# First routing round of a fused attention and MoE kernel: float digits, split counts, a table of zero matmuls, and a new order of the experts' work

## The chip, the cores and the metric

One core of a Trainium2 chip runs the whole program. The metric is the device time in microseconds, the median of the runs shown; the profile is one further execution, whose trace gives every duration used below. TensorE is called PE, VectorE DVE, ScalarE ACT, GpSimd POOL and SyncE SP, as in the rows.

## The reference, cut to what matters

```python
# attention: 4 batches, 8 heads, 768 positions, 64 wide; sink of 4 keys and a window of 128
attn = softmax(mask(q @ k.T / 8)) @ v
x = attn.transpose(0, 2, 1, 3).reshape(3072, 512)
logits = x @ w_gate                      # 3072 tokens, 8 experts
order = argsort(-logits.flatten())
for idx in order:                        # greedy, capacity 384 for each expert
    tok, e = idx // 8, idx % 8
    if assigned[tok] >= 0 or counts[e] >= 384: continue
    assigned[tok] = e; counts[e] += 1
for e in range(8):
    out[assigned == e] = relu(x[assigned == e] @ w1[e]) @ w2[e]     # 512 -> 1024 -> 512
```

The greedy loop is done in eight rounds. In each the expert that fills up first is found, with the threshold at which its 384th token is taken; its tokens leave the pool, and the round hands over an expert number and 384 row numbers.

## The kernel before

The first stretch of the program is attention over 24 chunks of 128 positions, in an order written out by hand (`SEQ`). It leaves the rows x in DRAM and the logits `L` (128 partitions x 24 chunks x 8 experts) in SBUF. `Moe.side` puts the first operations of the first routing round, over the first 18 of the 24 columns, into that order as `pr0` to `pr16`.

The second stretch is planned: `graph` adds every instruction of the eight rounds (`phase`, classes R0 to R7), of the gathers and transposes of rows (`rows`, G and X), of the weights (`weights`, L, H, W) and of the two matmul layers (`mlp`, M and N) to a `Graph`, each with a cost and with what it reads and writes. `Graph.order` is a list scheduler: it takes the ready instruction of best rank, shifted by a number for each class from the table `BIAS`, within a window `WIN`. Each engine then runs its instructions strictly in the order that comes out. `run` emits them.

A round (`phase`, L420) looks for the threshold digit by digit. The best logit of each token is made into a sortable integer by `prep` (L376): `v` (L381) is the maximum, `vm` adds a penalty for tokens already taken, `f` and `s` (L386, L388) make the integer, `di` (L390 to L398) and `df` (L399) its digits, `w`, `mx` and `oh` (L385 to L393) the one-hot best expert. There are six steps, `STEPS`, two with 64 digit values and four with 32 (numbered 0 to 5 below: 64, 64, 32, 32, 32, 32). In each, `compare` (L356, L359) sets `cmp` to digit >= grid value for all 24 columns; `gather` (L375) counts for each expert, by matmuls with `cmp` as weights and `oh` as the moving operand, into the PSUM bank `pr`. DVE compares the counts with 384 (`odd`, `two`, `odd`, `i`: L458 to L463), one matmul `dp` (L467) sums over the partitions, and DVE reads it as the digit `P` (L469) and subtracts it (`xb`, L470; `x` and `y`, L450 to L452). With 32 values the layout before puts four column groups in one count, 6 matmuls of 128 weights and 32 columns, and the two halves of the result need the extra pair `odd`, `two` (L458, L459). After step 5 come the mask `M` (L482), running counts `sc` (L485), the ranks (L488, L489), `q` (L493), then the slot of each token in its expert's list, compared with 64 low values (`lo`, L498, L356) and six 64-wide edges in fp32 (L505, L509, L510), a last count (`pick`, L375), and the row numbers `idx` (L517 to L520). POOL gathers three times 128 rows with them (L557), PE transposes them (L565), ACT and DVE split them in a high and a low part `xh`, `xl` (L567, L568), and the first layer starts (L578, L586 for the first two column blocks, L581 for the others; the second layer is L597).

While PE waits in the first round it runs matmuls of zeros (`warm`, L418): `WARM` gives the number before each count, into the same bank `pr` as the count, and `run` adds more in the gaps of its own plan, into `ph`.

Weights come in 64 chunks of 512 KB over two raw buffers (`raw`, L548): ACT copies the high part `wh` (L550), DVE makes the low part `wl` (L552), and only then is the raw buffer free. Chunk 2 of the first expert also waits for the gathered rows.

The lines that put zeros ahead of a count before the change:

```python
for n,(sh,m) in enumerate(STEPS):
    ...
    def counts(n=n,m=m,cnt=cnt,z=z,h=h,j=j):
        if first: self.warm(cnt,WARM[n])
        self.gather(cnt,j,m,self.oh,k)
```

Of the kernel before, what the change touches and what calls it, by code (L numbers as in the profile page):

```python
# [233 lines left out]
CAP=384  # L234

RUN=[(4,0)]*2+[(2,2)]*6
# [70 lines left out]
class Moe:  # L307
# [4 lines left out]
    def __init__(self,ctx,tc,L,idn):  # L312
        nc=tc.nc; self.tc=tc; self.nc=nc; self.L=L; self.idn=idn
# [20 lines left out]
        for n,dt in (('v',F32),('vm',F32),('f',I32),('s',I32),('mx',F32),('y',F32),('sl',F32),('m3',F32),('lo',I16),('si',I16),('x0',F32),('x1',F32),('xb0',BF),('xb1',BF)): setattr(self,n,t([128,NC],dt,n))  # L334
# [4 lines left out]
        self.M=t([128,2,NC],BF,"M"); self.xae=t([128,2,NC],F32,"xae"); self.sc=t([128,2*NC],BF,"sc"); self.q=t([128,2,NC],F32,"q"); self.c4=t([128,NC,7],F32,"c4"); self.edge=t([128,6],F32,"edge")  # L339
        for j in range(6): g.memset(self.edge[:,j:j+1],64.0*j+63.5)  # L340
        self.R=t([128,NC,6],F32,"R"); self.R3=t([128,NC,6],F16,"R3")
# [21 lines left out]
    def gather(self,out,j,m,y,k,dt=BF):  # L363

        z=128//m; U=RUN[k][m<64]; n=y.shape[2]; l=[]
        if U:
            for b in range(0,NC//U,z):
                q=min(z,NC//U-b)
                st=self.cmp[j][:,b*m*U:(b+q)*m*U].bitcast(dt).rearrange("p (x u) -> p u x",u=U); mv=y[:,b*U:(b+q)*U].rearrange("p (j u) e -> p u j e",u=U)
                l+=[(q*m,q*n,st[:,u],mv[:,u]) for u in range(U)]  # L370
        else:
            st=self.part(j,m).bitcast(dt); mv=y.rearrange("p (j c) e -> p c j e",j=z)
            l=[(128,z*n,st[:,:,c],mv[:,c]) for c in range(NC//z)]
        l=[l[0]]+[x for x in l if x[0]<128]+[x for x in l[1:] if x[0]==128]
        for i,(r,w,a,b) in enumerate(l): self.nc.tensor.matmul(out[0:r,0:w],a,b,start=i==0,stop=i==len(l)-1)  # L375
    def prep(self,k,a,b):  # L376
# [13 lines left out]
            (u(n/2),lambda: V.tensor_scalar(di[:,5],s,-2**31,26,op0=OP.bitwise_xor,op1=OP.logical_shift_right),'s','di5'),  # L390
            (u(n/2),lambda: V.tensor_scalar(di[:,0],s,-2**31,20,op0=OP.bitwise_xor,op1=OP.logical_shift_right),'s','di0'),
            (u(n/2),lambda: V.tensor_copy(self.xb0[:,c],di[:,5]),'di5','xb0'),
            (u(8*n),lambda: V.tensor_tensor(self.oh[:,c],w,wide(mx),OP.is_equal),'w1 mx','oh'),  # L393
            (u((56 if RUN[k][0]==2 else 32)*n),lambda: self.compare(0,self.xb0,64,a,b,k),'xb0','cmp0'),
# [21 lines left out]
    def warm(self,bank,n):  # L416

        for _ in range(n): self.nc.tensor.matmul(bank[:,128:512],self.onesb,self.grid[:,0:16,:].rearrange("p m c -> p (m c)"),start=True,stop=True)  # L418

    def phase(self,g,k):  # L420
# [7 lines left out]
        if not last:  # L428
# [3 lines left out]
            if a<NC:  # L432
                for c,fn,r,w in self.prep(k,a,NC): v(c,fn,r,w)
            xb=(self.xb0,self.xb1); xs=(self.x0,self.x1); x,xn=self.df[:,0],'df'
            for n,(sh,m) in enumerate(STEPS):
                cnt,bn=bank(); j=n%2; cn=f'cmp{j}'; z=128//m; h=NC//z
                if n: v(u(NC*m/(1.15 if RUN[k][m<64]==2 else 2)),lambda j=j,m=m: self.compare(j,xb[j],m,0,NC,k),f'xb{j}',cn)
                def counts(n=n,m=m,cnt=cnt,z=z,h=h,j=j):
                    if first: self.warm(cnt,WARM[n])

                    self.gather(cnt,j,m,self.oh,k)
                e({0:62*h if m==64 else 52*h,2:27*h,4:35*h}[RUN[k][m<64]]+(100 if first else 0),counts,cn+' oh'+(' m0go' if (k,n)==(1,1) else ''),bn,f'cnt{n}')
# [13 lines left out]
                if z==2: top,tn=cnt[0:64,0:E],bn  # L456
# [10 lines left out]
                e(60,lambda z=z,dp=dp,wt=wt: nc.tensor.matmul(dp[:,0:E],wt,self.i8[z//4],start=True,stop=True),f'i8{z//4}',bn,f'dp{n}')  # L467
# [36 lines left out]
        v(u(NC),row0,'M0','c40')
        v(u(6*NC),lambda: V.tensor_tensor(c4[:,:,1:7],sl[:,:,None].to_broadcast([128,NC,6]),self.edge[:,None,:].to_broadcast([128,NC,6]),OP.is_ge),sn,'c4')  # L505
        oj=0; on=f'cmp{oj}'
        ip,bn=bank()
        v(u(NC*(56 if RUN[k][0]==2 else 32)),lambda: self.compare(oj,self.lo,64,0,NC,k,OP.is_equal,F16),'lo',on)
        v(u(6*NC),lambda: V.tensor_tensor(R,c4[:,:,0:6],c4[:,:,1:7],OP.subtract),'c40 c4','R')  # L509
        v(u(6*NC),lambda: V.tensor_tensor(self.R3,R,self.tid[:,:,None].to_broadcast([128,NC,6]),OP.mult),'R','R3')  # L510
        def pick():
            if first: self.warm(ip,WARM[6])
            self.gather(ip,oj,64,self.R3,k,F16)
# [100 lines left out]
    def run(self):  # L614
# [114 lines left out]
```

## Time and profile before

| | |
|---|---|
| three runs | 478.36, 478.58, 485.38 us |
| median | 478.58 us |
| profiled execution | 480.82 us, of which the span of the trace is 479.1 us |
| busy over the span | PE 442.8 us (92%), DVE 372.9 us (78%), ACT 227.2 us (47%), POOL 153.9 us (32%) |

Times in rows are counted from the start of the span; 1.72 us of the profiled execution lie outside it. A row of the timeline gives the start, the duration, the engine, the line, the operation, what it writes and reads, and in square brackets the idle time of the engine before it with what ended it. Merged rows end in xN and cover from the first start to the last end.

### The profile page before, as it was taken

The page shows a single profiled execution, that of the slowest core. Times are in us where ns is not written, and L with a number is a line of the kernel's source. Part 1 is how long each engine was busy: PE and PEld are TensorE (multiplying, and loading weights), DVE is VectorE, ACT ScalarE, POOL GpSimd, SP SyncE. Part 2 cuts the span into 40 slices and gives each one's busy share as a digit, 9 for nine tenths or more (in the row PEclk, how much of TensorE's full clock was granted, in tenths as well). Part 3 has the DMA queues.
Part 4 walks back from the last instruction along what each step waited for, and adds up shares of the span by engine and source line. Part 5 has one row for each costly group of instructions (what it writes and reads, how often), then busy time and mean ns, then how long its engine had stood idle before and what let it go on. Part 6 is the DMA issues. An engine that isn't in the chain of part 4 may idle for free.

```text
span 479.1 us, 14064 instructions
## 1 busy us (share of the span) xinstructions
PE 442.8 (92%) x5464; PEld 366.4 (76%) x5468; DVE 372.9 (78%) x1147; ACT 227.2 (47%) x647; POOL 153.9 (32%) x297
## 2 busy tenths in 40 slices
PE   9899898999864989999999999999999999999994
PEld 5587786877741578778879879878987889988983
DVE  5799898899886889988999989988878986463210
ACT  4988788789600153353344244335234345363110
POOL 5696667669800200411321211122031033011001
PEclk9999999899985699999999999999999999999999
DMA  8647658475620552572474463364346166664001
GB/s 280 204 139 217 214 180 258 136 220 160 197 73 0 176 156 89 175 234 74 129 224 132 136 216 134 110 200 153 110 136 189 73 203 229 190 194 153 0 23 44
DMA packets 44875, 73.79 MB, mean 154 GB/s; under 512 B 3592, under 2 KB 21256, under 8 KB 44808
## 3 DMA queue, kind: packets, MB, share of 16 engines
q1 hardware_dynamic: 40536, 59.78, 39.8%
q0 software_dynamic: 3840, 12.59, 7.7%
q8 instruction: 43, 0.70, 0.6%
q10 hardware_dynamic: 432, 0.52, 0.4%
q14 instruction: 24, 0.20, 0.1%
HBM read 60.28 MB, written 12.60 MB: 152 GB/s over the span
## 4 chain that ended last, share of the span: by engine, by line
PE 51%; DVE 27%; DMA 8%; ACT 6%; issue 5%; POOLq 0%; POOL 0%; SPq 0%; DVEq 0%; ACTq 0%
PE ph L581 17%; PE py L597 16%; DMA raw<-w 7%; DVE wl L552 5%; PE pp L147 4%; PE pp L93 3%; ACT P L24 3%; DVE cmp L356 3%; PE pr L375 2%; DVE pp L106 2%; PE pp L156 2%; DVE xt L160 2%; ACT wh L550 2%; DVE hl L589 2%; PE ph L418 1%
## 5 line engine op out<-in xcount | busy, mean ns | idle before, releaser
L550 ACT ACTIVATE wh<-raw 128x1024 fp32r<-128x1024 f32 x64 | 67.8, 1061 | 86.9 <-DMA raw<-w 58.7
L552 DVE TENSOR_TENSOR wl<-raw,wh 128x1024 fp32r<-128x1024 f32 x64 | 78.0, 1220 | 18.9 <-ACT wh L550 18.4
L581 PE MATMUL ph<-xh,wh 128*128 128x384 f32 x248 | 87.4, 352 | 0.0
L581 PE MATMUL ph<-xh,wl 128*128 128x384 f32 x248 | 83.7, 337 | 0.0
L581 PE MATMUL ph<-xl,wh 128*128 128x384 f32 x248 | 83.5, 337 | 0.0
L597 PE MATMUL py<-wh,hh 128*128 128x512 f32 x192 | 79.0, 411 | 0.0
L557 POOL DMA_INDIRECT xg<-x_dram,idx x24 | 30.1, 1254 | 149.1 <-issue 50.5
L597 PE MATMUL py<-wh,hl 128*128 128x512 f32 x192 | 75.4, 393 | 0.0
L597 PE MATMUL py<-wl,hh 128*128 128x512 f32 x192 | 75.3, 392 | 0.0
L24 ACT ACTIVATE P<-pp,nmx 128x136 f32<-128x136 f32 x192 | 69.4, 387 | 11.7 <-DVE nmx L107 10.1
L602 POOL DMA_INDIRECT out<-yo,idx x24 | 29.6, 1232 | 133.4 <-ACT yo L600 103.0
L588 ACT ACTIVATE hh<-ph 128x384 fp32r<-128x384 f32 x64 | 31.3, 489 | 85.1 <-PE ph L581 72.8
L589 DVE SCALAR_TENSOR_TENSOR hl<-ph,hh 128x384 fp32r<-128x384 f32 x64 | 34.9, 552 | 21.2 <-ACT hh L588 20.7
L581 PEld LDWEIGHTS ph<-xh,wh 128*128 128x128 f32 x248 | 46.8, 189 | 2.3 <-issue 0.4
L581 PEld LDWEIGHTS ph<-xl,wh 128*128 128x128 f32 x248 | 46.7, 188 | 1.6
L93 PE MATMUL pp<-kk,q 64*64 64x204 f32 (+2 forms) x768 | 43.8, 334 | 4.0 <-issue 3.2
L581 PEld LDWEIGHTS ph<-xh,wl 128*128 128x128 f32 x248 | 46.6, 188 | 0.0
L597 PEld LDWEIGHTS py<-wh,hl 128*128 128x128 f32 x192 | 36.0, 188 | 8.4 <-DVE hl L589 0.4
L24 ACT ACTIVATION_READ_ACCUMULATOR P<-pp,nmx 128x1 f32 x192 | 42.2, 220 | 0.0
L597 PEld LDWEIGHTS py<-wh,hh 128*128 128x128 f32 x192 | 36.2, 189 | 5.9 <-issue 1.6
L597 PEld LDWEIGHTS py<-wl,hh 128*128 128x128 f32 x192 | 36.2, 189 | 4.2
L135 POOL TENSOR_TENSOR E<-PT,me 128x256 f32<-128x256 f32 x48 | 34.6, 731 | 14.5 <-ACT PT L24 14.5
(169 smaller groups left out, 780.5 us busy)
## 6 DMA issues: line engine op xcount, KB each, us to landing
raw<-w SPq DMA_DIRECT2D x64, 512.0 KB, 3.7
kk<-kd SPq DMA_DIRECT2D x23, 272.0 KB, 3.1
v<-vd SPq DMA_DIRECT2D x24, 256.0 KB, 3.0
x_dram<-xt SPq DMA_DIRECT2D x24, 256.0 KB, 4.6
q<-qd SPq DMA_DIRECT2D x22, 256.0 KB
vx<-vs SPq DMA_DIRECT2D x1, 432.0 KB, 4.9
xg<-x_dram,idx POOLq DMA_INDIRECT x24
out<-yo,idx POOLq DMA_INDIRECT x24
```

The source lines that it names most:

```text
L24: def act(*a,**k): last[:]=[nc.scalar.activation(*a,**k)]
L93: PE.matmul(sp[o,s,260*u+a:260*u+204],q[p,2*g+u,o],kk[p,2*i-2+f+a//68:2*i+f+1,2*g+u],start=True,stop=True)
L135: def op_A(c,g): G.tensor_tensor(T('E',c)[:,2*g:2*g+2],diag(c,g),me[:,None].to_broadcast([128,2,2,64]),OP.mult)
L147: PE.matmul(av[half(s),u,a:a+64*n],T('v',c-w)[half(u),256*l+64*x:256*l+64*x+64],m.rearrange("p a n->p (a n)"),start=g==0 and n==2 and w==0 ...
L550: g.add('A',947,lambda wh=wh,raw=raw: nc.scalar.activation(wh,raw,AF.Copy),[f'raw{q}'],[f'wh{s}'],f'H{k}.{j}',f'W{k}')
L552: g.add(e,{'V':1160,'P':2303}[e],lambda wh=wh,wl=wl,raw=raw,e=e: (nc.vector if e=='V' else nc.gpsimd).tensor_tensor(wl,raw,wh.bitcast(F32) ...
L557: g.add('P',1650 if k<4 else 1200,lambda t=t: nc.gpsimd.indirect_dma_start(out=self.xg[t],out_offset=None,in_=self.x_dram,in_offset=bass.I ...
L581: nc.tensor.matmul(p[:,0:CAP],x[:,c,:],y[:,c,:],start=c==0 and i==0,stop=c==3 and i==2)
L588: g.add('A',371,lambda f=f,p=p: nc.scalar.activation(self.hh[:,f,:],p[:,0:CAP],AF.Relu),ps,[f'hh{f}'],f'hh{k}.{f}',f'H{k}')
L589: g.add('V',469,lambda f=f,p=p: nc.vector.scalar_tensor_tensor(self.hl[:,f,:],p[:,0:CAP],0.0,self.hh[:,f,:].bitcast(F32),op0=OP.max,op1=OP ...
L597: nc.tensor.matmul(p,x[:,f,ts],w,start=f==0 and i==0,stop=f==7 and i==2)
L602: st=nc.gpsimd.indirect_dma_start(out=self.out,out_offset=bass.IndirectOffsetOnAxis(ap=idx[:,t:t+1],axis=0),in_=y,in_offset=None)
```

## The change

- `prep`, `compare0`: in the first round step 0 compares the fp32 logits `v` themselves with 64 fp32 `edges` (made once at the start of the program), so that `di5` and `xb0` are left out there; the result goes to `cmp` in bf16 as before.
- `RUN[0]` is (4,4): in the first round also the 32-value steps keep their columns in groups of four. All counts there take two column groups (z=2), 12 matmuls of 128 weights and 16 columns; `odd`/`two` at L458 and L459 fall away, the weights read are 128 wide, and with 32 values half of the output rows are not used.
- In the first round `compare` is cut in two parts (columns 0 to 15 and 16 to 23), and so is each count (8 + 4 matmuls with 64 values, 4 + 8 with 32).
- All rounds: `c4` and `R` become 16-bit (`tm`, `hi`, `R`, `R3`; L512 to L524 after), `sl` and the six edges fall away.
- The zero matmuls come from a table `FILL` by the name of the instruction they precede, all into `ph`; the gap rule in `run` and `WARM` fall away.
- `rehearse`: one indirect DMA of 128 rows of 512 bytes from `ident` into a tile that nothing reads.
- `BIAS` and `WIN` have new values, which change the order of all eight experts' work.

The diff, cut to its core:

```diff
-RUN=[(4,0)]*2+[(2,2)]*6
+RUN=[(4,4),(4,0)]+[(2,2)]*6
...
+        self.edges=t([128,64],F32,"edges"); w=self.edges.bitcast(I32); f=t([128,64],I32,"ef"); V=nc.vector
+        g.iota(f,pattern=[[1,64]],base=-32,channel_multiplier=0)
+        V.tensor_scalar(w,f,26,None,op0=OP.logical_shift_left)
+        V.tensor_scalar(f,w,31,0x7fffffff,op0=OP.arith_shift_right,op1=OP.bitwise_and)
+        V.tensor_tensor(w,w,f,OP.bitwise_xor)
+        g.memset(self.edges[:,0:1],-3.0e38)
+        self.row=t([128,1],I32,"row"); self.dum=t([128,128],F32,"dum")
...
+    def compare0(self,a,b):
+
+        a//=4; b//=4; n=b-a
+        o=self.cmp[0].rearrange("p (t m u) -> p t m u",m=64,u=4)[:,a:b]; x=self.v[:,4*a:4*b].rearrange("p (t u) -> p t u",u=4)
+        self.nc.vector.tensor_tensor(o,x[:,:,None,:].to_broadcast([128,n,64,4]),self.edges[:,None,:,None].to_broadcast([128,n,64,4]),OP.is_ge)
...
-    def gather(self,out,j,m,y,k,dt=BF):
+    def gather(self,out,j,m,y,k,dt=BF,z=None,part=None):
...
-        l=[l[0]]+[x for x in l if x[0]<128]+[x for x in l[1:] if x[0]==128]
-        for i,(r,w,a,b) in enumerate(l): self.nc.tensor.matmul(out[0:r,0:w],a,b,start=i==0,stop=i==len(l)-1)
+        l=[l[0]]+[x for x in l[1:] if x[0]<l[0][0]]+[x for x in l[1:] if x[0]==l[0][0]]
+        n=len(l); c=8 if m==64 else 4; lo,hi=(0,n) if part is None else (0,c) if part==0 else (c,n)
+        for i,(r,w,a,b) in list(enumerate(l))[lo:hi]: self.nc.tensor.matmul(out[0:r,0:w],a,b,start=i==0,stop=i==n-1,skip_group_check=part is not None)
...
-            (u((56 if RUN[k][0]==2 else 32)*n),lambda: self.compare(0,self.xb0,64,a,b,k),'xb0','cmp0'),
+            (u((56 if RUN[k][0]==2 else 32)*n),lambda: self.compare(0,self.xb0,64,a,b,k),'xb0','cmp0'+(' cmp0a cmp0b' if k==1 else '')) if k else (u(64*n),lambda: self.compare0(a,b),'v','cmp0'),
...
+                if n and first:
+                    for a,b,h_ in ((0,16,'a'),(16,NC,'b')): v(u((b-a)*m/2),lambda j=j,m=m,a=a,b=b: self.compare(j,xb[j],m,a,b,k),f'xb{j}',cn+h_)
...
+                if first:
+                    e(280 if m==64 else 140,lambda c=counts: c(0),(cn+'a' if n else '' if self.done>=16 else cn+' oh'),bn,f'cnt{n}a')
+                    e(140 if m==64 else 280,lambda c=counts: c(1),bn+(f' {cn}b' if n else f' {cn} oh'),bn,f'cnt{n}')
...
+        v(u(NC),row0,'M0','c4')
+        v(u(NC),lambda: V.tensor_tensor(self.tm,c4,self.tid,OP.mult),'c4','tm')
...
+            v(u(NC/2),lambda: V.tensor_scalar(self.hi,self.si,6,None,op0=OP.logical_shift_right),'si','hi')
...
+        v(145,lambda: V.tensor_tensor(self.R,wide(self.hi),self.grid[:,0:6,:],OP.is_equal),'hi','R')
+        v(145,lambda: V.tensor_tensor(self.R3,self.R,wide(self.tm),OP.mult),'R tm','R3')
+        if first:
+            eq(0,16,'lo R3',on+'a'); eq(16,NC,'lo',on+'b')
...
+    def rehearse(self):
+
+        g=self.nc.gpsimd; g.iota(self.row,pattern=[[0,1]],base=0,channel_multiplier=1)
+        g.indirect_dma_start(out=self.dum,out_offset=None,in_=self.ident,in_offset=bass.IndirectOffsetOnAxis(ap=self.row,axis=0))
     def run(self):
         g=self.graph(); self.g=g
         o=g.order(BIAS,WIN,{})
...
+        self.rehearse()
+        for _,i,_ in sorted(o):
             t=g.t[i]
             if t[2] is None: continue
+            self.warm(FILL.get(t[4],0))
             t[2]()
...
-WARM=[2, 2, 2, 1, 1, 1, 3]
-WIN=[77, 803571, 2155]
+FILL={'R0.cnt0': 5, 'R0.dp0': 2, 'R0.cnt1a': 7, 'R0.dp1': 2, 'R0.cnt2a': 4, 'R0.dp2': 2, 'R0.cnt3a': 4, 'R0.dp3': 2, 'R0.cnt4a': 4, 'R0.dp4': 2, 'R0.cnt5a': 4, 'R0.dp5': 2, 'R0.pp': 6, 'R0.ipa': 10, 'R1.cnt0': 31, 'R1.dp0': 2, 'X0.0.0': 4, 'X0.0.1': 5, 'M0.0.0': 1}
+WIN=[158.873, 47573.645, 42.308]
```

Three places show how the instructions stand.

On DVE, step 2 of the first round (32 values) in the kernel before; `pr` is the bank of counts, `odd`, `two` and `i` lead to the matmul `dp`, whose sum is `P`:

```order
L470 TENSOR_TENSOR xb_104<-x_103,P_118 128x24
L451 SCALAR_TENSOR_TENSOR x_102<-P_118,y 128x24
L359 TENSOR_TENSOR cmp_110<-xb_104,grid 128x768
L450 SCALAR_TENSOR_TENSOR y<-x_102,df 128x24
L458 TENSOR_SCALAR odd<-pr_3250 64x16
L459 TENSOR_TENSOR two<-pr_3250,odd 64x16
L462 TENSOR_SCALAR odd<-two 32x8
L463 SCALAR_TENSOR_TENSOR i_113<-two,odd 32x8
L469 TENSOR_REDUCE P_117<-pr_3250 128x1
```

The same step on DVE in the changed kernel:

```order
L485 TENSOR_TENSOR xb_104<-x_103,P_118 128x24
L362 TENSOR_TENSOR cmp_110<-xb_104,grid 128x512
L362 TENSOR_TENSOR cmp_110<-xb_104,grid 128x256
L466 SCALAR_TENSOR_TENSOR x_102<-P_118,y 128x24
L465 SCALAR_TENSOR_TENSOR y<-x_102,df 128x24
L477 TENSOR_SCALAR odd<-pr_3251 32x8
L478 SCALAR_TENSOR_TENSOR i_113<-pr_3251,odd 32x8
L484 TENSOR_REDUCE P_117<-pr_3251 128x1
```

The compare now follows `xb` directly and is cut in two, `x` has moved behind it, and two of the four small operations between count and `dp` are gone.

On PE, from the end of a `dp` matmul to the next count, in the kernel before (step 2; `onesb` and `grid` are the zeros' operands):

```order
L467 MATMUL pr_3250<-i_112,wt_71 128x8
L418 LDWEIGHTS onesb
L418 MATMUL pr_3250<-grid,onesb 128x384
L418 LDWEIGHTS onesb
L418 MATMUL pr_3250<-grid,onesb 128x384
L375 LDWEIGHTS cmp_110
L375 MATMUL pr_3250<-oh,cmp_110 128x32
```

The same place (from `dp` of step 2 to the count of step 3) in the changed kernel:

```order
L430 LDWEIGHTS onesb
L430 MATMUL ph_3247<-grid,onesb 128x384
L482 LDWEIGHTS wt_71
L482 MATMUL pr_3251<-i_113,wt_71 128x8
L430 LDWEIGHTS onesb
L430 MATMUL ph_3247<-grid,onesb 128x384
L430 LDWEIGHTS onesb
L430 MATMUL ph_3247<-grid,onesb 128x384
L430 LDWEIGHTS onesb
L430 MATMUL ph_3247<-grid,onesb 128x384
L430 LDWEIGHTS onesb
L430 MATMUL ph_3247<-grid,onesb 128x384
```

Four zero matmuls stand between `dp` and the first part of the next count, two more ahead of `dp`, and they write to `ph`, which no DVE instruction of the round reads.

On POOL, the start of the program in the kernel before, with the semaphores that an instruction waits for (`full` is a triangle, `m_200`, `mprev` and `m_201` are the attention's masks):

```order
L50 AFFINE_SELECT full<-one 128x128 [waits DVE_49]
L51 COPY m_200<-full 64x64 [waits Pool_49]
L51 COPY m_200<-full 64x64
L52 MEMSET m_200 64x4 [waits Pool_49]
L53 COPY mprev<-full 64x64 x2
L54 MEMSET m_201 64x4
```

The same place in the changed kernel:

```order
L50 AFFINE_SELECT full<-one 128x128 [waits DVE_49]
L630 IOTA row 128x1
L51 COPY m_203<-full 64x64 [waits Pool_49] x2
L631 DMA dum<-ident,row 128x128 [waits Pool_49]
L348 MEMSET edges 128x1 [waits DVE_49]
L52 MEMSET m_203 64x4
L53 COPY mprev<-full 64x64
L53 COPY mprev<-full 64x64 [waits DMASW0_49,Pool_49]
L54 MEMSET m_204 64x4
```

The indirect DMA of `rehearse` has come to stand here, in the first microseconds of the program, and the second half of `mprev` waits for the semaphore of POOL's own DMA queue, that is for its landing.

## Rows read from the trace of the kernel before

**Rows 1.** Busy time by stretch: window, length, busy by engine, PEclk, DMA share, GB/s.

```profile
138.12:168.97 30.85, 19.61 (x143) 10.72 (x141) 23.58 (x115) 2.60 (x4) 3.10 (x3) 0.61 0.28 88
140.00:163.00 23.00, 13.33 (x85) 6.24 (x86) 17.04 (x87) 2.06 (x2) 2.16 (x3) 0.50 0.17 56
168.97:472.37 303.40, 298.76 (x1837) 257.66 (x1837) 233.00 (x673) 119.76 (x180) 55.60 (x44) 1.00 0.46 144
```

**Rows 2.** Timeline, steps 0 to 2 of the first round.

```profile
138.16 0.20 DVE L381 TENSOR_REDUCE v<-L 128x6 f32<-128x48 f32 x1
...
140.28 0.18 DVE L399 CAST df<-di 128x30 f32<-128x30 int32 x1
140.49 0.17 DVE L462 TENSOR_SCALAR odd<-pr 64x8 f32<-64x8 f32 x1
...
141.31 0.18 DVE L470 TENSOR_TENSOR xb<-df,P 128x24 bf16<-128x24 f32 x1
...
141.53 0.96 DVE L356 TENSOR_TENSOR cmp<-xb,grid 128x1536 bf16<-128x1536 bf16 x1
...
143.97 0.18 DVE L470 TENSOR_TENSOR xb<-x,P 128x24 bf16<-128x24 f32 x1
...
144.18 0.56 DVE L359 TENSOR_TENSOR cmp<-xb,grid 128x768 bf16<-128x768 bf16 x1
...
145.30 0.18 DVE L458 TENSOR_SCALAR odd<-pr 64x16 f32<-64x16 f32 x1 [0.46 <-PE pr L375]
...
145.71 0.16 DVE L462 TENSOR_SCALAR odd<-two 32x8 f32<-32x8 f32 x1
...
146.51 0.18 DVE L470 TENSOR_TENSOR xb<-x,P 128x24 bf16<-128x24 f32 x1
```

**Rows 3.** Timeline, DVE: a bf16 compare and an fp32 subtraction of 1024 columns.

```profile
133.27 0.69 DVE L356 TENSOR_TENSOR cmp<-xb,grid 128x1024 bf16<-128x1024 bf16 x1
...
163.77 1.23 DVE L552 TENSOR_TENSOR wl<-raw,wh 128x1024 fp32r<-128x1024 f32 x1
```

**Rows 4.** Timeline, from the ranks of the first round to its gathers.

```profile
155.53 0.21 DVE L493 TENSOR_TENSOR q<-pr,M 128x48 f32<-128x48 f32 x1 [0.20 <-PE pr L489]
...
156.31 0.95 DVE L356 TENSOR_TENSOR cmp<-lo,grid 128x1536 f16<-128x1536 int16 x1
...
157.51 0.31 DVE L510 TENSOR_TENSOR R<-R,tid 128x144 f16<-128x144 f32 x1
157.87 0.54 PE L375 MATMUL pr<-R,cmp 128*128 128x12 f16 x12 [0.97 <-DVE R L510]
...
159.01 0.17 DVE L520 TENSOR_TENSOR idx<-pr,sw 64x3 int32<-64x3 f32 x1
...
160.23 1.17 POOL L557 DMA_INDIRECT xg<-x_dram,idx  x1 [28.08 <-DVE v L381]
```

**Rows 5.** Timeline, gather of a later round: row numbers; and chain of waits: gather to landing.

```profile
196.24 0.17 DVE L520 TENSOR_TENSOR idx<-pr,sw 64x3 int32<-64x3 f32 x1
...
197.14 5.30 DMA xg<-x_dram,idx
```

**Rows 6.** Timeline, from the second round's first compare to the first layer.

```profile
162.16 0.96 DVE L356 TENSOR_TENSOR cmp<-xb,grid 128x1536 bf16<-128x1536 bf16 x1
...
165.12 1.46 PE L418 MATMUL ph<-grid,onesb 128*128 128x384 bf16 x8
...
168.97 0.44 PE L578 MATMUL ph<-xh,wh 128*128 128x384 f32 x1 [0.25 <-ACT xh L567]
```

**Rows 7.** Timeline, the attention's masks at the start: POOL makes one, DVE uses it.

```profile
3.79 0.50 POOL L53 COPY mprev<-full 64x64 int32<-64x64 int32 x2
...
8.98 0.43 DVE L100 COPY_PREDICATED pp<-mprev,pp 128x256 f32<-128x256 int32 x1
```

**Rows 8.** PE within the layers: chain of waits, 63 matmuls in a row; timeline, a wait.

```profile
439.17 10.95 PE ph L581 x63
...
175.47 0.45 PE L375 MATMUL pr<-oh,cmp 128*128 128x32 bf16 x6 [1.01 <-DVE cmp L359]
```

More of the change, by code (lines that the diff above doesn't have):

```diff
@@ L307, with __init__ @@
 class Moe:
[L312 to L313 removed]
+    def __init__(self,ctx,tc,L,idn,ident):
+        nc=tc.nc; self.tc=tc; self.nc=nc; self.L=L; self.idn=idn; self.ident=ident
         c=self.rc=ctx.enter_context(tc.tile_pool(name="rc",bufs=1))
@@ L415, in pools, with warm @@
         self.nr=0; self.regs={}; self.sc_=[]
-    def warm(self,bank,n):
-        for _ in range(n): self.nc.tensor.matmul(bank[:,128:512],self.onesb,self.grid[:,0:16,:].rearrange("p m c -> p (m c)"),start=True,stop=True)
+    def warm(self,n):
+        for _ in range(n): self.nc.tensor.matmul(self.ph[1][:,128:512],self.onesb,self.grid[:,0:16,:].rearrange("p m c -> p (m c)"),start=True,stop=True)
     def phase(self,g,k):
@@ L432, in phase, with counts @@
             if a<NC:
-                for c,fn,r,w in self.prep(k,a,NC): v(c,fn,r,w)
+                for c,fn,r,w in self.prep(k,a,NC):
+                    if k or w not in ('di5','xb0'): v(c,fn,r,w)
             xb=(self.xb0,self.xb1); xs=(self.x0,self.x1); x,xn=self.df[:,0],'df'
             for n,(sh,m) in enumerate(STEPS):
[L436 to L442, printed above, removed]
+                cnt,bn=bank(); j=n%2; cn=f'cmp{j}'; z=2 if first else 128//m; h=NC//(128//m)
+                if n and first:
+                    for a,b,h_ in ((0,16,'a'),(16,NC,'b')): v(u((b-a)*m/2),lambda j=j,m=m,a=a,b=b: self.compare(j,xb[j],m,a,b,k),f'xb{j}',cn+h_)
+                elif n: v(u(NC*m/(1.15 if RUN[k][m<64]==2 else 2)),lambda j=j,m=m: self.compare(j,xb[j],m,0,NC,k),f'xb{j}',cn+(f' {cn}a {cn}b' if k==1 else ''))
+                def counts(part=None,m=m,cnt=cnt,z=z,j=j): self.gather(cnt,j,m,self.oh,k,z=z,part=part)
+                if first:
+                    e(280 if m==64 else 140,lambda c=counts: c(0),(cn+'a' if n else '' if self.done>=16 else cn+' oh'),bn,f'cnt{n}a')
+                    e(140 if m==64 else 280,lambda c=counts: c(1),bn+(f' {cn}b' if n else f' {cn} oh'),bn,f'cnt{n}')
+                else: e({0:62*h if m==64 else 52*h,2:27*h,4:35*h}[RUN[k][m<64]],counts,cn+' oh'+(' m0go' if (k,n)==(1,1) else ''),bn,f'cnt{n}')
                 if n:
@@ L506, in phase @@
         oj=0; on=f'cmp{oj}'
         ip,bn=bank()
[L508 to L513, printed above, removed]
-        e({0:740,2:310,4:425}[RUN[k][0]]+(100 if first else 0),pick,on+' R3',bn,'ip')
+        wide=lambda x: x[:,None,:].to_broadcast([128,6,NC]); R3=self.R3.rearrange("p m c -> p c m")
@@ new lines, in phase @@
+        eq=lambda a,b,r,w: v(u((b-a)*(56 if RUN[k][0]==2 else 32)),lambda: self.compare(oj,self.lo,64,a,b,k,OP.is_equal,F16),r,w)
+        if not first: eq(0,NC,'lo',on+(f' {on}a {on}b' if k==1 else ''))
+        v(145,lambda: V.tensor_tensor(self.R,wide(self.hi),self.grid[:,0:6,:],OP.is_equal),'hi','R')
+        v(145,lambda: V.tensor_tensor(self.R3,self.R,wide(self.tm),OP.mult),'R tm','R3')
+        if first:
+            eq(0,16,'lo R3',on+'a'); eq(16,NC,'lo',on+'b')
+            for part,h_ in ((0,'a'),(1,'b')): e((280,140)[part],lambda part=part: self.gather(ip,oj,64,R3,k,F16,part=part),on+h_+' R3'+(' '+bn if part else ''),bn,('ipa','ip')[part])
+        else: e({0:740,2:310,4:425}[RUN[k][0]],lambda: self.gather(ip,oj,64,R3,k,F16),on+' R3',bn,'ip')
```

58 lines of the change are left out of this document (22 added, 36 removed).

## The prediction

> **What bounds the kernel now.** I read busy time by stretch first. The reader is to see three numbers there [rows 1]. In the layers, from 168.97 to the end of PE's work at 472.37, PE is busy for 298.76 of 303.40 us at a granted clock of 1.00: PE is the bound, and no more than 4.64 us can be won by any order of instructions. From 138.12 to 168.97, the first round and its gathers, PE is busy for 19.61 of 30.85 us and DVE for 23.58, and neither is the bound: a chain of small operations runs to and fro between them. [...] So the change can act in four places: at the start of the program (the new indirect DMA), in the 30.85 us, in the 4.64 us, and by disturbing the layers.
>
> The timeline of the steps came next [rows 2]. A step of 64 values takes 2.66 us (from the subtraction `xb` at 141.31 to the next at 143.97), one of 32 values 2.54 (143.97 to 146.51). The four steps of 32 values repeat within .01. In each the path is `xb`, `cmp`, count, `odd`, `two`, `odd`, `i`, `dp`, `P`, `xb`. Then come the end of the round [rows 4], the same place in a later round [rows 5], the second round and the first layer [rows 6], the start [rows 7] and PE inside the layers [rows 8].
>
> **The change part by part.** All terms are against the profiled execution, 480.82 us.
>
> *Steps of 32 values, four of them.* L458 and L459 go: from 145.30 to 145.71 is .41 [rows 2]. The count becomes 12 matmuls of 16 columns in the place of 6 of 32; 12 of 12 columns took .54 [rows 4] and 6 of 32 took .45 [rows 8], so +.09. Against this the count starts on the first part of `cmp`. Compares take .56 for 768, .69 for 1024 and .96 for 1536 columns [rows 2, 3], that is .13 for 256, so the part of 512 columns ends .14 earlier than the compare of before, and the second part some .1 later than it. The 8 matmuls behind the second part take two thirds of .54, or .36. So the count ends at .1 + .36 after the old end of the compare, where it was .45: +.01. Taken up with a little for the extra instruction: −.38 for a step, −1.5 for four. Bounds: −1.9 (the cut costs nothing, .48 each) and 0. The bound of 0 is where the four zeros between `dp` and the count run at the lower clock: at the full rate 8 zeros take 1.46 us [rows 6], .18 each or less, and four of them .7, which lies beside `P`, `xb` and the first part of the compare (.20 + .21 + .42 = .83). At half the rate they would take 1.4 and end some .4 behind that. [...]
>
> *Step 1, 64 values.* Only the cut in two parts acts. Before, 12 matmuls stood behind a compare of .96 [rows 2]; now 8 have run when the second part (512 columns) ends and 4 are left. That is two thirds of .54 less, .36, minus .1 to .15 for the second instruction: −.2 (−.3 to 0).
>
> *Step 0.* The compare itself no longer needs the integer. `di5` and `xb0` go, but `s`, the other `di` and `df` (the last ends at 140.46, .03 before `odd` [rows 2]) now stand behind `i`, in the time of `dp`, where DVE had idled, and `P` and `xb` wait for them. I take +.3 (−.2, if the earlier `odd` is all that counts, to +.5).
>
> *End of attention.* Compares of fp32 over 18 columns stand now in the stretch where DVE is the busier engine. An fp32 operation of 1024 columns took 1.23 and the bf16 compare of 1024 took .69 [rows 3]; most of the added time lies earlier, under attention, and only the last 16 columns near 138 hurt: +.2 (0 to +.3).
>
> *Ranks to row numbers.* From `q` (155.53) to `idx` (159.01) is 3.48 us [rows 4]. The second compare is cut in parts, and the products with `tid` (.31) become 16-bit and stand ahead of it: I take −.3 for the row numbers (−.6 to 0) and −.1 for `sc`, which stands earlier, together −.4.
>
> *The first gather.* It starts 1.22 after its row numbers [rows 4], a later round's .90 after [rows 5]. If the .32 is a first use, the rehearsal takes it: −.3 (−.32 to 0).
>
> *The start.* The rehearsal's DMA has come to stand in the first 4 us of POOL, and the second half of `mprev`, in one row with the first at 3.79 before, waits until it has landed. DVE needs `mprev` at 8.98 [rows 7]. No row shows a landing there. The nearest is 5.30 from the start of a gather to its landing [rows 5], which carries four times the bytes. From a start near 3.7, 5.30 ends at 9.0, and the copy adds .25: 9.25, .27 late. With some delay passed on I take +.4 (0, if it lands in half that time, to +3.6, if it takes half as long again and all behind it waits).
>
> *From the gathers to the first layer.* `idx` comes .4 + 1.5 + .2 − .3 − .2 earlier, 1.6 less the start's .4, and the gather .3 more: −1.5. Two rows limit what follows: from `idx` (159.01) to the second round's first compare was 3.15 us (162.16), and the first layer begins at 168.97 [rows 4, 6]. In the new order PE runs the second round's first count and `dp` before the first rows' transposes, with 31 and more zeros, so DVE's part of the second round lies closer to the path: +.2. The first layer would start 1.3 us earlier, at 167.7.
>
> *The layers.* The matmuls are the same in number and size, 63 in 10.95 us, .174 each [rows 8], and at the bound PE gives only the idle 4.64 back. In the new order 6 matmuls (1.04 us) stand between `dp` and the next count in the second round's steps where DVE needs about 1.25: some +1.2 over the round. In other rounds 6 to 9 of the second layer's stand where 3 did, and waits such as the 1.01 before a count [rows 8] shrink: −1.2. I take 0 (−3 to +3; all of 4.64 doesn't go, since the first layer's start is part of it).
>
> The sum: +.4 + .2 + .3 − .2 − 1.5 − .4 − .3 + .2 + 0 = −1.3, so 479.5 for an execution like the profiled one. That execution stands 2.24 us (.5%) above the median of 478.58; the same loss set against the median gives 477.3.
>
> [...]
>
> **The rivals.**
> *The new order also removes waits.* If half of the layers' 4.64 us goes [rows 1], 2.3 more, and the rest is as summed, the time is 477.3 − 2.3 = 475.0. For it: waits of 1.01 before a count [rows 8] would fill with a longer piece of the second layer. Against it: the second round, where the steps stand closer.
> *The layers give it back.* DVE falls behind in the second round (+1.2) and the other rounds gain nothing: 478.5.
> *Slower: the rehearsal holds up the start.* One mechanism, on POOL: the DMA issued near 3.7 lands late, since attention's first loads are under way, and `mprev` with it. Then L100 on DVE waits, and behind it all of the first chunks' softmax. If the landing takes 8 us, `mprev` is there at 3.7 + 8 + .25 = 11.95, 3.0 after 8.98. With the other terms of −1.7 that is +1.3: 479.9 against the median. It decides from a landing of about 6.7 us on, where the delay reaches 1.7. For it: 5.30 for a gather, in a calmer place [rows 5]. Against it: it moves 64 KB, a gather 256 KB.
> *The first use only moves.* If the .32 at the first gather [rows 4, 5] is paid in POOL at the start, ahead of `mprev`, what the gather saves is lost there: 477.3 + .3 = 477.6. That is all that the rows give it.
> *The clock stays at the lower level.* Then four zeros outlast the compare: the four steps gain nothing (+1.5), and the longer rows of zeros ahead of the ranks cost about as much again: 477.3 + 3 = 480.3. For it: 23 us at .50 [rows 1]. Against it: PE would then have next to no idle time, and it had 9.67 us in those 23.
>
> **How the numbers follow.** Forecast .42; waits removed .20; layers give it back .17; rehearsal late .11; clock low .06; first use only moves .02; others .02. The likeliest gives 477.3. The range takes the bounds of the layers and of the start: 473 (4.3 lower: waits removed, and the steps at their bound) to 481 (the rehearsal at nearly its upper end). Two per cent, 9.6 us, is about what a measurement of this kernel can tell from no change; no case reaches it, and a gain of that size would need more than all of the 4.64 and a sixth of the first round. So within 2% has .95, faster .03, slower .02.
>
> **What would show it.** Right: steps of about 2.17 us with `odd` once in each; a granted clock near 1.00 from 140 to 163; row numbers to gather .9; a first layer near 167.7 plus or minus the start; L100 within .5 of 8.98; PE's idle time in the layers near 4.6. Wrong: L100 at 12 or later, zeros that end behind the compare, a first layer later than 169, or idle time in the layers below 2.5 or above 6.

## The result, and the profile after

Over 20 executions of each kernel the changed one takes 482.65 us (median) and the one before 480.23. The ratio is 1.0065, with a 95% interval from 1.0042 to 1.0088: slower by .65%, inside 2%, and on the other side of the forecast (477.3 against 478.58, a ratio of .9973). The profiled execution took 482.61, its span is 480.9.

Busy time by stretch of the changed kernel, with the columns of [rows 1]:

```profile
135.87:165.31 29.44, 24.17 (x213) 14.06 (x211) 24.19 (x109) 2.66 (x4) 2.92 (x3) 1.00 0.26 83
140.00:160.00 20.00, 17.05 (x152) 9.71 (x152) 15.48 (x74) 1.32 (x2) 2.92 (x3) 1.00 0.23 73
165.31:474.04 308.73, 300.95 (x1837) 258.14 (x1837) 230.01 (x675) 120.23 (x180) 58.41 (x44) 0.99 0.44 143
```

The first round runs at a granted clock of 1.00 where it had .50, and from the last logits to the first layer it takes 29.44 us where it took 30.81 (138.16 to 168.97) [rows 2, 6]. The layers, though, take 308.73 us for the same 1837 matmuls that took 303.40 [rows 1]: PE is idle for 7.78 us in them, where it was for 4.64, and busy for 2.19 more.

The steps of the first round on DVE, changed kernel (timeline):

```profile
135.87 0.20 DVE L393 TENSOR_REDUCE v<-L 128x6 f32<-128x48 f32 x1
...
139.12 0.18 DVE L485 TENSOR_TENSOR xb<-df,P 128x24 bf16<-128x24 f32 x1
...
141.65 0.18 DVE L485 TENSOR_TENSOR xb<-x,P 128x24 bf16<-128x24 f32 x1
141.87 0.63 DVE L362 TENSOR_TENSOR cmp<-xb,grid 128x512 bf16<-128x512 bf16 x2
...
143.02 0.16 DVE L477 TENSOR_SCALAR odd<-pr 32x8 f32<-32x8 f32 x1 [0.21 <-PE pr L387]
143.21 0.15 DVE L478 SCALAR_TENSOR_TENSOR i<-pr,odd 32x8 bf16<-32x8 f32 x1
...
143.82 0.18 DVE L485 TENSOR_TENSOR xb<-x,P 128x24 bf16<-128x24 f32 x1
```

A step of 32 values is 2.17 us (141.65 to 143.82), with one `odd` in it. Set beside [rows 2], count to `dp` has lost two instructions and little else has moved.

The start on POOL and DVE, changed kernel (timeline), beside [rows 7]:

```profile
3.81 1.15 POOL L631 DMA_INDIRECT dum<-ident,row  x1 [0.29 <-POOL m L51]
...
5.20 0.49 POOL L53 COPY mprev<-full 64x64 int32<-64x64 int32 x1
10.14 0.23 POOL L53 COPY mprev<-full 64x64 int32<-64x64 int32 x1 [4.46 <-DMA dum<-ident,row]
...
10.41 0.43 DVE L100 COPY_PREDICATED pp<-mprev,pp 128x256 f32<-128x256 int32 x1 [1.46 <-POOL m L54]
```

The second half of `mprev` isn't copied until the rehearsal has landed, and comes 6.3 us after the rehearsal's start. DVE's L100 comes at 10.41 where it came at 8.98.

What PE waits for inside the layers, changed kernel (waits: engine, tile, line, releaser, us in total, times, longest):

```profile
PE pt L579 <- DMA xg<-x_dram,idx: 3.6, 3, 1.8
PE pr L387 <- DVE cmp L362: 2.6, 4, 1.1
PE pr L482 <- DVE i L478: 0.9, 4, 0.3
PE py L611 <- DVE wl L566: 0.5, 1, 0.5
```

In the kernel before, the waits for compares were 2.0 us in all, and the largest wait of all was the 1.01 of [rows 8]:

```profile
PE pr L375 <- DVE cmp L359: 1.0, 1, 1.0
PE pr L375 <- DVE cmp L356: 1.0, 3, 0.4
```

The first line of the changed kernel is new: transposes wait for gathered rows, 3.6 us in all. In the kernel before they never did. The longest of these waits, in round 3, is worth following. The timeline of POOL, DVE and PE there:

```profile
270.12 1.35 POOL L571 DMA_INDIRECT xg<-x_dram,idx  x1 [18.18 <-issue]
271.76 3.56 POOL L571 DMA_INDIRECT xg<-x_dram,idx  x1 [0.30 <-issue]
...
271.74 1.53 DVE L362 TENSOR_TENSOR cmp<-xb,grid 128x1536 bf16<-128x1536 bf16 x1
...
273.27 1.22 DVE L566 TENSOR_TENSOR wl<-raw,wh 128x1024 fp32r<-128x1024 f32 x1
...
280.56 0.63 PE L579 MATMUL pt<-idt,xg 128*128 128x128 f32 x2 [1.82 <-DMA xg<-x_dram,idx]
```

Here a gather that starts with no long DVE instruction under way occupies POOL for .94 to 1.03 us. The second one here began .02 after the first compare of the next round, behind which a subtraction of weights followed with no gap, and it took 3.56. Its rows landed 8.76 us after its start, and PE stood for 1.82 us. What came after that is in the windows of 2 us (columns as above):

```profile
278.00:280.00 2.00, 0.74 (x4) 0.26 (x2) 0.92 (x3) 1.06 (x1) 1.46 (x1) 1.00 0.70 142
280.00:282.00 2.00, 1.44 (x5) 1.09 (x5) 0.00 (x0) 0.00 (x0) 0.00 (x0) 0.67 0.58 186
282.00:284.00 2.00, 2.00 (x7) 1.44 (x6) 1.42 (x6) 0.00 (x0) 0.00 (x0) 0.50 0.48 192
284.00:286.00 2.00, 2.00 (x16) 1.62 (x16) 1.75 (x4) 1.05 (x3) 0.00 (x0) 0.98 0.00 0
```

After PE's pause the granted clock falls from 1.00 to .50, and PE, busy again, works at half its rate until about 284: two matmuls of 512 columns start .43 us apart there (281.42 and 281.85), and .23 behind it (284.17 and 284.40). Of 6 us (280 to 286) at .67, .50 and .98 the shortfall is 2 x (.33 + .50 + .02), or 1.7 us: most of the 2.19 that PE was busy for longer.

### The profile page after: what moved, and what is told of

It is laid out like the page before. It is cut to its first block, busy times and chain, and to the rows that moved or that the text cites. A ratio compares the mean times of both kernels' runs of the same rounds, so it can differ in the third digit from the quotient of the medians.

```text
span 480.9 us, 14216 instructions
## 1 busy us (share of the span) xinstructions
PE 447.3 (93%) x5541; PEld 368.0 (77%) x5541; DVE 369.6 (77%) x1145; ACT 227.7 (47%) x647; POOL 157.6 (33%) x295
## 4 chain that ended last, share of the span: by engine, by line
PE 43%; DVE 23%; issue 12%; DMA 11%; ACT 8%; POOL 1%; POOLq 0%; DVEq 0%; ACTq 0%; SPq 0%
PE ph L595 15%; PE py L611 14%; DMA raw<-w 5%; ACT P L24 4%; DMA xg<-x_dram,idx 4%; DVE wl L566 4%; PE pp L147 4%; DVE cmp L362 2%; PE pp L93 2%; ACT PT L24 2%; PE pr L387 2%; PE pt L579 2%; PE pp L156 2%; DVE xt L160 1%; DVE pp L106 1%
## 5 line engine op out<-in xcount | busy, mean ns | idle before, releaser
L571 POOL DMA_INDIRECT xg<-x_dram,idx x24 | 35.3, 1472 | 144.8 <-issue 35.4
L611 PE MATMUL py<-wh,hh 128*128 128x512 f32 x192 | 80.6, 420 | 0.0
L616 POOL DMA_INDIRECT out<-yo,idx x24 | 27.0, 1124 | 139.0 <-ACT yo L614 121.2
L603 DVE SCALAR_TENSOR_TENSOR hl<-ph,hh 128x384 fp32r<-128x384 f32 x64 | 34.9, 552 | 25.1 <-ACT hh L602 24.6
L93 PE MATMUL pp<-kk,q 64*64 64x204 f32 (+2 forms) x768 | 42.5, 327 | 4.0 <-issue 1.7
```

The source lines that it names most:

```text
L93: PE.matmul(sp[o,s,260*u+a:260*u+204],q[p,2*g+u,o],kk[p,2*i-2+f+a//68:2*i+f+1,2*g+u],start=True,stop=True)
L571: g.add('P',1650 if k<4 else 1200,lambda t=t: nc.gpsimd.indirect_dma_start(out=self.xg[t],out_offset=None,in_=self.x_dram,in_offset=bass.I ...
L603: g.add('V',469,lambda f=f,p=p: nc.vector.scalar_tensor_tensor(self.hl[:,f,:],p[:,0:CAP],0.0,self.hh[:,f,:].bitcast(F32),op0=OP.max,op1=OP ...
L611: nc.tensor.matmul(p,x[:,f,ts],w,start=f==0 and i==0,stop=f==7 and i==2)
L616: st=nc.gpsimd.indirect_dma_start(out=self.out,out_offset=bass.IndirectOffsetOnAxis(ap=idx[:,t:t+1],axis=0),in_=y,in_offset=None)
```

## The experiments

All ratios are to the kernel before, with their intervals, against executions on the same chip.

**Order and rehearsal, first set.**

```diff
 e1:   BIAS, WIN of the kernel before, in the changed kernel
 e2:   BIAS, WIN of the changed kernel, in the kernel before
 e3:   changed kernel
-        self.rehearse()
 e4:   e1 and e3 together
```

> The changed kernel with BIAS and WIN of the kernel before; all its other edits stay. Theory 1 (the new order of the experts' work costs about 5 us in the layers, because transposes stand too close behind the gathers, while the first round gains about 2.5 net of the start): ratio to the kernel before about 0.995, PE's idle time between the first layer's start and its last matmul near 4.6 us instead of 7.8, no wait of a transpose for gathered rows above 1 us. Rival 1 (the order is harmless; the loss is the rehearsal at the start and the rest is scatter of single executions): ratio about 1.006, as with the changed kernel.

> The kernel before with BIAS and WIN of the changed kernel and nothing else. Theory 1: slower by 4 to 5 us, ratio about 1.01, with PE waits for gathered rows in the layers. Rival 1: ratio 1.000 within its interval. A third reading (the new order only suits the shorter first round): slower by more than theory 1 says, ratio above 1.015.

> The changed kernel without the rehearsal (its iota and its indirect DMA are not issued; nothing reads their result). Theory 1: the second half of the mask mprev no longer waits; the start is 1.4 us shorter, the first gather starts some .1 later behind its row numbers, and the ratio falls from 1.0065 to about 1.004. Rival 1: the rehearsal is the loss, ratio about 1.000 or below.

> The changed kernel with the old BIAS and WIN and without the rehearsal: the edits of the first round alone. Theory 1: faster than the kernel before by 3.5 to 4 us, ratio about 0.992. Rival 1: same as without the rehearsal alone, ratio about 1.000.

Measured: e1 1.0047 (1.0007 to 1.0087), e2 1.0211 (1.0154 to 1.0269), e3 .9995 (.9961 to 1.0029), e4 .9981 (.9950 to 1.0011). e2 shows that the new order is costly without the other edits: there transposes and layers wait for rows and for splits, and PE is idle for 8.56 of the layers' 310.74 us. At 10 us it lies above 1.015, where the third reading stood (the new order suits only the shorter first round), so it isn't the order's price in the changed kernel. In e3, without the rehearsal, the loss is gone, which rival 1 had said (its repeat, f2 below, has 1.0024). e1 and e4 miss theory 1: the old table gives little back. The reason lies in the planner: with the changed costs of the first round the same table no longer gives the same order. Some 400 of TensorE's matmuls stand elsewhere than in the kernel before, and the layers of e4 take 306.03 us, not 303.40, with a fall of the clock behind one wait of 1.75 us (PE is busy for 300.69 us, before for 298.76). So a table put back isn't an order put back.

**The order kept.** In e5 the layers are emitted in the order that the kernel before had, read from its plan and held to the changed kernel's dependences.

```diff
 e5:   changed kernel without the rehearsal
-        o=g.order(BIAS,WIN,{})
+        o=kept(g)          # by the place of each instruction in the plan before
 e6:   e5 with the rehearsal
 e7:   e5 with the rehearsal, row<-L[:,0,0:1]*0+(0 to 127), issued at chunk 5
 e8:   e5
-FILL={'R0.cnt0': 5, ...}
+FILL={}
```

> The changed kernel without the rehearsal, its layers emitted in exactly the order that the kernel before had (read from that kernel's plan; on TensorE, ScalarE and SyncE only the first round differs). Run with the old table of numbers the planner had not given back that order, since the changed costs of the first round moved some 400 of TensorE's matmuls. Theory 2 (the layers cost more because any new order opens waits, the old one being nearly without): the first layer starts 1.4 to 1.8 us earlier than before counted from the last part of the logits, PE's idle time in the layers is near 4.6, ratio about 0.994. Rival 2 (the layers can't use an earlier start, since the weights arrive at their own pace): ratio 0.998 to 1.000, as with the old table.

> The same with the rehearsal at the start of the program, as in the changed kernel. Theory 2: the rehearsal costs what the two pairs of runs showed, 0.0066 and 0.0070, so ratio about 1.001. Rival 2: only the 1.2 us that the mask mprev comes late, 0.0025.

> The same with the rehearsal's rows made from a logit of an early chunk (times zero, so the rows are the same), so that its DMA is issued inside attention and no mask waits for it. Two small DVE instructions come on top. If the wait of mprev is the cost: ratio as without the rehearsal, about 0.994 and no more than 0.001 above it; the first gather starts 0.1 to 0.3 us sooner behind its row numbers. If the DMA itself is the cost (its descriptors, its queue): ratio about 1.001 as with the early one.

> The same as the kept order without the rehearsal, with an empty table of zero matmuls (no zeros run in the first round). Theory 2 on the clock: steps of the first round stay at 2.16 us, since the chain and not the rate of the matmuls sets them, the granted clock falls to .50 from about 140 on, and the first layer pays some 1 to 3 us at the lower rate: ratio 0.003 to 0.006 above the kept order. Rival: the zeros are worth nothing, same ratio within 0.001.

Measured: e5 .9925 (.9892 to .9959), e6 .9962 (.9919 to 1.0006), e7 .9940 (.9906 to .9974), e8 .9924 (.9886 to .9962). e5 is faster than both kernels. On PE its 1837 matmuls of the layers stand in the order of before without exception. Its stretch of layers:

```profile
164.87:467.69 302.82, 298.89 (x1837) 257.55 (x1837) 231.52 (x674) 119.88 (x180) 57.95 (x44) 1.00 0.45 144
```

So the layers can use an earlier start in full (rival 2 falls). e6 and e7 tell little apart by time. By profile, L100 waits .75 us for `mprev` in e6 and not at all in e7, and the first gather follows its row numbers by 1.11 us in e6 and 1.10 in e7, by 1.21 in e5: the rehearsal wins .1 there, wherever it stands. Nothing of it is left at the first layer, which comes 10.24, 10.21 and 10.21 us behind the row numbers in e6, e7 and e5.

In e8 the zeros are gone and the time is the same, against theory 2. The windows of e5 and of e8:

```profile
138.00:160.00 22.00, 19.07 (x175) 10.97 (x173) 17.45 (x87) 2.12 (x2) 3.10 (x3) 1.00 0.22 70
```

```profile
138.00:160.00 22.00, 5.75 (x91) 4.08 (x92) 17.53 (x91) 2.06 (x2) 2.56 (x3) 0.55 0.19 61
```

The clock is .55 without the zeros, and DVE does the same work in the same time. From the last logits to the first layer e8 needs 28.31 us, e5 29.12: it has no zeros to finish between the transposes. The layers of e8 are longer by 2.1, with PE busy .9 longer (from their start to the DVE instruction `P` at 169.11 it is 4.14 us, in e6 3.38) and idle 1.2 longer (one wait of 2.2 us for an `i`, at 298).

The zeros can also cost. Step 1 of the first round on PE, in the changed kernel and in f3 (a run of the last set below, with the same zeros):

```profile
138.32 1.30 PE L430 MATMUL ph<-grid,onesb 128*128 128x384 bf16 x7
140.16 0.63 PE L387 MATMUL pr<-oh,cmp 128*128 128x16 bf16 x12 [0.54 <-DVE cmp L362]
```

```profile
139.95 2.40 PE L430 MATMUL ph<-grid,onesb 128*128 128x384 bf16 x7
142.14 0.58 PE L387 MATMUL pr<-oh,cmp 128*128 128x16 bf16 x12
```

In f3 the granted clock is .50 from 139.1 to 142.5. The seven zeros take 2.40 us instead of 1.30, and the count waits for them and not for its compare. The clock falls like this somewhere in the first round in nine of the fifteen profiles with these zeros, and in seven of them step 1 takes 2.81 to 3.25 us. In the other eight it takes 2.52 to 2.54, and in e8, at .50 and without zeros, 2.53.

**Gathers behind a long DVE instruction.**

```diff
 e9:   e3, on DVE in rounds 4 and 6
-  cmp<-xb,grid    di    wl<-raw,wh
+  di    wl<-raw,wh    cmp<-xb,grid
 e10:  e3, all of X3 and X5 later by 2.5 us in the plan
```

> The changed kernel without the rehearsal, with its new order, but the first compares of rounds 4 and 6 moved one place down on DVE, behind the next subtraction of weights (their counts on TensorE move a few matmuls down with them). Theory 3 (a gather on POOL that is issued while a long two-input instruction runs on DVE is locked out until that ends; 3.56 and 3.39 us in place of .96 where compare and subtraction stand back to back): the second gather of round 3 and the first of round 5 take 1.0 to 1.4 us, the waits of transposes for gathered rows (1.12 and 1.31 us in the run without the rehearsal) fall below 0.3, and the ratio falls from 0.9995 by 0.002 to 0.005. Rival 3 (the gathers are slow because weights are loaded at the same time): they still take over 3 us, ratio unchanged.

> The same kernel with the compares where the new order has them, but the transposes of rounds 3 and 5 set 2.5 us later in TensorE's order. Both theories: the gathers stay slow (3.56 and 3.39 us) and the waits of transposes vanish. If these waits, with what follows them, are what the new order costs: ratio lower by 0.002 to 0.005 than without the rehearsal (0.9995). If the cost lies in the many small waits for DVE in the new order: no change.

Measured: e9 .9986 (.9958 to 1.0013), e10 1.0131 (1.0086 to 1.0176). In e9 the second gather of round 3 is short, with the compare no longer ahead of it:

```profile
273.33 0.98 POOL L571 DMA_INDIRECT xg<-x_dram,idx  x1 [0.30 <-issue]
274.61 2.25 POOL L571 DMA_INDIRECT xg<-x_dram,idx  x1 [0.30 <-issue]
...
273.39 1.22 DVE L566 TENSOR_TENSOR wl<-raw,wh 128x1024 fp32r<-128x1024 f32 x1
274.52 1.51 DVE L362 TENSOR_TENSOR cmp<-xb,grid 128x1536 bf16<-128x1536 bf16 x1
```

At 273.33 the gather came .06 ahead of a subtraction and took .98, while that subtraction ran. The next came .09 behind the compare and took 2.25, that is the compare's rest of 1.42 and .83 more. So it isn't the load on the DMA engines that makes a gather long on POOL: of these two, the one that started ahead of the DVE instruction wasn't held, the one behind it was. In the traces of both kernels and of e1 to e8 the 77 gathers that began with no long DVE instruction (over .4 us) under way took .94 to 1.17. In all 18 traces 210 gathers began while a compare or a subtraction of weights had .2 us or more to run. Of these, 194 ended .82 to .93 behind its end and 14 were held by the next one as well; the two that weren't held had begun within .01 of it. `hl` (L603 after), which reads one input from PSUM, held none of nine, though it had .4 to .5 us to run. The compares and subtractions read both inputs from SBUF; why they hold a gather, no run here shows.

The next instruction doesn't always hold the gather. In 41 cases a second compare or subtraction followed within .04 us, and it held the gather in 13 of them; a fourteenth came .15 us behind and held it too (e8). What decides isn't shown. So the same place of the same order can cost 3.39 us in the changed kernel (round 5) and 2.21 in f1:

```profile
347.05 2.21 POOL L571 DMA_INDIRECT xg<-x_dram,idx  x1 [14.19 <-issue]
```

Round 5's first gather kept its 3.39 in e9, since the subtraction now stood in the compare's place; but it no longer made PE wait. All waits of transposes for rows in the layers fell from 2.4 us (e3) to 0.2, as theory 3 had it. The time fell by no more than the intervals allow: the layers are 1.0 us shorter (305.14 for 306.10), and e9's counts wait longer for the moved compares (2.5 us in place of 2.0). What is shown is where the long gathers come from; that their removal pays isn't shown. e10, where neither reading expected a loss, shows that later transposes are no cure: the layers grow to 312.39 us, with 1.6 us of waits for the high part of rows (`xh`) that then come too late.

**Repeats, and the square.** e11 and e12 are e5 and e6 again. f1 to f4 put both parts side by side on one chip: f1 the changed kernel, f2 it without the rehearsal (as e3), f3 the kept order (as e5), f4 the kept order with the rehearsal (as e6).

> The kept order without the rehearsal once more, for a second estimate and a second profile. Theory 2: ratio 0.9925 within 0.003, the first layer 29.1 us behind the last part of the logits, PE's idle time in the layers below 5.

> The kept order with the rehearsal once more. If the rehearsal costs what the first profile shows, half a microsecond to one at the mask: ratio 0.001 to 0.0025 above the kept order; if it costs what the two earlier pairs of times showed: 0.0066 above.

> The changed kernel itself. If the two parts add (order 0.006, rehearsal 0.003): ratio 1.003 to 1.007.

> The changed kernel without the rehearsal. If the rehearsal costs what masks and first chunks show in the profiles (0.5 to 1.5 us): 0.001 to 0.003 below the changed kernel; if it costs what the first two pairs of times showed: 0.006 to 0.007 below.

> The changed kernel without the rehearsal, with the layers in the order of the kernel before. If the order costs what the profiles show in the layers (302.8 and 303.3 us against 306.1): 0.005 to 0.007 below the same kernel in the new order, ratio 0.993 to 0.996.

> The same with the rehearsal: above the kept order by the rehearsal's cost, 0.001 to 0.003 by the profiles, 0.006 to 0.007 by the first two pairs.

Measured: e11 .9962 (.9925 to .9998), e12 .9957 (.9920 to .9994), f1 1.0054 (1.0020 to 1.0089), f2 1.0024 (.9990 to 1.0058), f3 .9945 (.9909 to .9981), f4 .9960 (.9929 to .9990). In the square the new order costs .0079 (f2 over f3) and .0094 (f1 over f4), 3.8 to 4.5 us, and the rehearsal .0030 (f1 over f2) and .0015 (f4 over f3), .7 to 1.4 us. The order's cost is clear of the noise of such a pair. The rehearsal's isn't, pair by pair: its six pairs, e11 and e12 among them, lie between -.0005 and .0070. Their mean is .0036, some 1.7 us. In the six profiles with the rehearsal at the start L100 begins between 9.67 and 10.57, in those without it between 8.98 and 9.53. That this delay is the whole cost is argued: the last logits come at 135.87 to 138.49 with it and at 135.75 to 140.80 without it, so single executions don't show it there. What is left for all other edits together is f3 itself, -.0055 or 2.6 us.

Waits of PE in the layers of f3, to be set beside those of the changed kernel:

```profile
PE pt L579 <- DVE xl L582: 1.2, 1, 1.2
PE pr L482 <- DVE i L478: 1.0, 3, 0.4
PE py L611 <- DVE hl L603: 0.2, 1, 0.2
```

The layers took 308.73, 306.10, 304.17 and 308.74 us in the four profiles of the new order (the changed kernel, e3, f1, f2), 306.9 on average, and 301.44 to 304.98, on average 302.6, in the seven of the kept order with zeros (e5, e6, e7, e11, e12, f3, f4). The difference of 4.3 us is the order's cost in times, within their intervals. By the averages of these profiles PE is idle for 3.0 us more in the new order and busy for 1.4 more. It waits 2.2 us for gathered rows (.1 in the kept order) and 2.0 for compares (.2). The clock takes .9: it fell in two of the four profiles, in the changed kernel behind a wait of 1.82 us for rows, in f2 behind one of 1.94 us for an `i`.

f1's round 3 has the same gather of 3.56 us, but no wait for rows. From the gather's start to the landing of its rows, in the changed kernel and in f1 (chain of waits):

```profile
271.76 8.76 DMA xg<-x_dram,idx
```

```profile
272.33 6.98 DMA xg<-x_dram,idx
```

The gather is late by the same 2.6 us in both, and the transfer behind it took 1.8 longer in the first; why isn't shown. The order leaves so little room that some executions lose the 3 us and others don't. And waits for rows aren't all of its cost: f1 without them and e9 with .2 of them still have layers of 304.2 and 305.1 us, for 302.6.

## Why the prediction was wrong

Steps 2 to 5 were right: 2.17 us each, as worked out (2.54 less .38), -1.5 in all. In the other profiles with the zeros, steps 2 to 4 take 2.16 to 2.18, but for one of 2.37 in f1. From the last logits to the row numbers the profile has 19.08 us (135.87 to 154.95) for 20.85, -1.8, and the terms for these steps summed to -1.8: step 0 cost +.1 where +.3 stood, step 1 gave -.13 for -.2, ranks to row numbers (from `q`, 151.67) 3.28 for 3.48 us, -.2 for -.3. The end of attention cost nothing that shows, not +.2: the two parts of `v` lie 16.04 us apart (119.83 to 135.87), 16.10 before, and 15.0 to 17.5 in the other profiles. The clock stood at 1.00 from 140 to 160, as the term for these steps needs. That six zeros a step hold it there was the author's estimate, and no run shows it: with the same zeros the clock fell within the round in nine of fifteen profiles. Then what the rival on the clock named, zeros that outlast the compare, happened to the seven of step 1 and once to the four of a later step (1.44 us for .81, in f1).

The first gather gained .1, not .3: its row numbers are at 154.95 and it starts at 156.06. The step that failed there took the whole .32 for a first use. From gather to first layer .5 was lost (8.74 to 9.25 us), not .2. The zeros ahead of the transposes stand on that way: in the kept order it takes 9.00 us with them (e5) and 8.14 without (e8).

The start was a term of the sum that was mis-sized: +.4 was forecast, DVE's L100 came 1.4 us late. The landing was set by a gather's 5.30 and took 6.2. The slower rival named this mechanism and its place, and put 6.7 us as the point from which it would decide; the landing did not reach that. In the square the rehearsal costs .7 to 1.4 us, over all six pairs 1.7.

The step that failed is the one on the layers: "I take 0 (-3 to +3)". It set +1.2 for PE's queue between the second round's steps against -1.2 for waits that would shrink in other rounds. The profile has +5.3, the kept order's comparison +4.3. Waits like the 1.01 before a count did not shrink: the changed kernel waits 2.6 us for compares, the kernel before 2.0. And a wait came from a place that wasn't looked at, between POOL's gathers and the transposes behind them: 3.6 us, and 1.7 more for the clock behind it. How the order's cost divides between the two kinds of wait is told by profiles alone; e9 took the second away and the time did not show it.

Which DVE instruction would stand at a gather's start in the new order could be read from the order, and the rows that price it were in the trace of before:

```profile
199.26 1.53 DVE L356 TENSOR_TENSOR cmp<-xb,grid 128x1536 bf16<-128x1536 bf16 x1
199.32 2.30 POOL L557 DMA_INDIRECT xg<-x_dram,idx  x1 [0.30 <-issue]
```

This gather began .06 behind a compare and took 2.30 us, where others took .95. It cost PE nothing there. And no row stood behind the bound of +3: the 4.64 us bound what an order can win, not what it can lose.

The rival "the layers give it back" was nearest in kind, with +1.2; the measured loss is three to four times that. So the other edits earn 2.6 us, the order takes 3.8 to 4.5 and the rehearsal .7 to 1.4. In the square these give f1's own 2.6 by construction; the 20 executions of the result have 2.4.

The time of a single execution also moves by some us in attention, which the change doesn't touch: from L100 to the first part of `v` the profile after has 109.4 us (10.41 to 119.83), that of before 113.1 (8.98 to 122.06), and all 18 lie between 109.4 and 115.2. This hides much of the loss when the two spans are compared (480.9 and 479.1).

## What to carry to other kernels

When a change replaces the order of work in a stretch that is already at an engine's limit, what it can win is bounded by that engine's idle time, but what it can lose is not: each thin margin can open, and the clock can fall behind a pause (here 1.7 us behind a wait of 1.82). Price a new order by its margins, gather to transpose and compare to count, and by what stands on DVE where a gather starts (here up to 3.56 us on POOL for .95); and test a retuned order apart from the edits that came with it, by holding the order itself, since a planner's table doesn't hold it. A warm-up that other work must wait for has to be placed where nobody waits, and filling idle time with zeros is worth measuring first: they stand in the queue ahead of real work (here .9925 with them in e5, .9924 without in e8).

## What the runs showed of the hardware that was not expected

In these runs a gather on POOL was held up for as long as a compare or a subtraction of weights ran on DVE that had begun before it (194 of 210 gathers ended .82 to .93 us behind it), and sometimes, 14 times, by the next one too (3.56 and 3.39 us against .95), while one that began .06 ahead of a subtraction wasn't disturbed (.98). A wait of 1.82 us on PE was followed by some 3 us at a granted clock of .50; one of 2.2 us, in e8, left no such fall that shows: over all the layers PE is busy there for 299.75 us, in e6 for 298.76, and some .76 of the difference comes ahead of 169.11. And a first round at .55 of the clock, without zeros, took DVE's chain no longer than one at 1.00 (17.53 us of DVE work from 138 to 160 for 17.45, step 1 2.53 in e8 and in the changed kernel), while seven zeros at the lower clock (.50 in f3) held a count up by .3 to .7 us.
